# RWKV5 attention and a SwiGLU feed-forward layer on one core: VectorE's attention work of a late step in one line between the pieces, a quarter's silu products and later sums of h on GpSimd, and another order of the projections

## The chip, the cores and the metric

The kernel runs on one core of a Trainium2 chip. The core has a matrix engine (TensorE, PE in the profile, with its weight loads as PEld), a vector engine (VectorE, DVE), an activation engine (ScalarE, ACT), GpSimd (POOL), and a sync engine (SP), which in this kernel only issues DMAs. TensorE writes to PSUM, eight banks here; VectorE and ScalarE read PSUM and SBUF, and GpSimd is given work in SBUF alone. Each engine takes its instructions in the order in which the program emits them and waits at each for what it needs from the others. The metric is the device time of one execution in microseconds (us), the median of several.

## The reference

Two layers follow each other, all in float32. The first is a linear attention with a decaying state, over 4 batches, 8 heads, 768 positions and a head size of 48:

```
for t in range(S):
    cur = u * k_t (x) v_t
    y_t = r_t @ (state + cur)
    state = w * state + k_t (x) v_t
```

Its result, 3072 tokens by 384, goes into a feed-forward layer with 1536 hidden columns:

```
g = x @ w_gate
out = (silu(g) * (x @ w_val)) @ w_out
```

## The kernel before

**Attention.** The sequence is cut into chunks of 128 positions, one chunk of one batch to a step: 24 steps. From step 12 on (`PAIRED`) a step holds half a chunk of two batches at once. Step s works on several of them: it scales k and r for s+1 (`scale_k`, `scale_r`: GpSimd, L353 and L356), forms r·k·u for s+1 (`own_begin` L264, `own_end` L267: GpSimd) and its sum over a head (`own_sum` L275: VectorE), spreads that sum on diagonals (`diagonal` L376: eight ScalarE activations, which stand in a queue `small`), moves blocks of the scaled k and r (`move_blocks` L435: eight DMAs of SP's queue) and turns them (`turn_blocks` L456: two VectorE transposes, kT and rT). At one place in the step, called the *visit* in this document, TensorE does the outputs of s−2 (`paired_outputs` L557), the scores of s−1 (`paired_scores` L523) and the state update of s−2 (`paired_update` L571). Scores leave four masked copies for VectorE (L531), the update four sums into the state (L587), each second one followed by a product with the decay on GpSimd (L590). These eight wait in a deque `lazy`. `fill_turned` (SP) and `fill_own` (ScalarE's queue) are DMAs that fill the other parts of the score matrix `At`. Scores and update share four PSUM banks, the *ring*: a step takes three of the four in turn, so the second bank of this step's scores is the first bank of the last step's, and the third and fourth state sum read it.

**The feed-forward layer** is the bulk of TensorE's work, and it is cut into *pieces* that are fed between the parts of attention: a list `todo`, from which `feed` takes one at a time. With each piece `feed` also takes one from `lazy` (two while more than six are left) and up to three from `small`. From step 12 on, `gaps` feeds ten pieces in a step, two in each of five gaps: two pieces come before the visit and eight after it. One feeding is called a *turn* here, 1 and 2 before the visit, 3 to 10 after it. `turn_blocks` transposes kT after turn 3 and rT after turn 4; the sums of the state are taken in turns 6 to 9; the own sum comes ahead of turn 1 of the next step.

A *block* g = 2, 4, 6 holds 512 tokens (g and g+1, 256 each). Gate and value of a block come from `three_beside`: the 1536 columns are done in four quarters t = 0 to 3 of three tiles each, and each quarter is a fast multiplication of 15 products, *rounds* r0 to r14 (`three_step`, L924: four matmuls each). GpSimd forms the weight sums for it (`w_forms`, L854, and `in_place`, L827), VectorE the sums of x (`x_forms`, L881). Rounds add up in chains in PSUM: a bank is read out by VectorE or ScalarE (L948, called through `later`) after one round and then added to by the next of its chain, so the next must wait until the reading is done. These readings go to rows of `hv`: gates in their place, values in six rows at `place`. When a quarter is complete, ScalarE applies silu to its gates (L955) and a product with the values follows, for tile i = 0 and 1 on VectorE and for i = 2 on GpSimd (all L948); in quarter 3 there is one such product for each g instead, 128x768, the second as late as project 01. Quarter 1 has its values in rows 6 to 11, the other three in rows 0 to 5, so the readings of quarter 3 overwrite what the products of quarter 2 read.

The output projection is the 2x2 scheme with seven products, pieces "jn" of `two_projections`: j is the member of the pair, n the product (`project`, L740: twelve matmuls). Products 2 to 6 but 5 read sums of h (`h_sums`: L713 and L714 for the first pair of sums, L716 and L717 for the second). Their results are read out by ScalarE (L746, L750) and VectorE (L748, L753, L756) into two banks a and b of each g, b being written by product 1 and again by product 4 after L748 has read it. Product 1 reads tiles 6 to 11 of the first half of the tokens.

Pieces of one block fall on steps so: in steps 13, 17, 21 quarter 0 and most of quarter 1; in 14, 18, 22 the rest of it and quarter 2; in 15, 19, 23 the end of quarter 3 in turns 1 to 6 with project 00 in turn 5, then 10, 01, 02 and 11; in 16, 20, 24 the other projections 04 and 03 ahead of the visit, 12 and the rest after it, with the next block's first rounds between. Blocks 8 and 10 follow behind the last step in a scheme of their own (from about 436 us in the profile).

Of the kernel before, what the change touches and what calls it, by code (L numbers as in the profile page):

```python
# [15 lines left out]
P = 128  # L16
# [6 lines left out]
def fast(  # L23
# [419 lines left out]
                        ),  # L443
                    )

    def turn_blocks(i):

        turned[i] = three.tile([P, HP, P], FP32, name="rT", tag="rT")
        merged = hats[:, 6:8].rearrange("p n h x -> p (n h x)").rearrange(
            "p (q n a x) -> p n q a x", q=4, n=2, a=HP  # L450
        )
        for n, (dst, src) in enumerate(((kT[i % 2], blocks[0]), (turned[i], blocks[1]))):
            if i < PAIRED:
                dve.transpose(dst[:].rearrange("p a (t q) -> p q a t", q=4), merged[:, n])
            else:
                dve.transpose(dst[:].rearrange("p a t -> p (a t)"), src)  # L456
            if dst is kT[i % 2]:
                feed(1)

    lazy = deque()  # L460

# [242 lines left out]
    def h_sums(g, n):  # L704
        h11, h12, h21, h22 = h_quarters(g)
        if g < THREES:
            t = three.tile([P, 2, FH, P], FP32, name="hs", tag="w_bits")
        else:
            t = room["hs"][2 * (g % 2) + n]
        x = part_of.setdefault(g, {})  # L710
        x["s"] = x.get("s", ()) + (t[:, 0], t[:, 1])
        if n == 0:
            dve.tensor_add(t[:, 0], h22, h21)  # L713
            dve.tensor_sub(t[:, 1], t[:, 0], h11)  # L714
        else:
            dve.tensor_sub(t[:, 0], h11, h21)  # L716
            dve.tensor_sub(t[:, 1], h12, x["s"][1])  # L717

    def project(g, n):

# [218 lines left out]
    def three_beside(g):  # L939
# [18 lines left out]
        for t in range(4):  # L958
# [8 lines left out]
            if t < 3:  # L967
# [43 lines left out]
            later(at["r8"] + 0.1, dve.tensor_add, c[3], c[3], "l8")  # L1011
            give(at["r8"] + 0.2, "l8")
            if t < 3:
                for i, on in enumerate((dve, dve, pool)):
                    silu(
                        *((z + 11.7, z + 11.8) if i == 2 else (z + 15.6 + i / 10, z + (16.2, 22.1)[i])),
                        hTs[:, :, 3 * t + i], values[:, :, i], on,
                    )
# [391 lines left out]
    round_act()  # L1410
    load(6)
    for s in range(4, N + 2):
        if 4 < s < N:
            own_sum(s)
        if PAIRED <= s < N:
            diagonal(s)
        late = BLOCKS < s + 1 < N and s % 2 == 0
        if s + 3 == PAIRED:
# [7 lines left out]
            turn(s)  # L1426
        if s + 1 < N:
            scale_k(s + 1)
            if s < LATE:
                if not late:  # L1430
                    scale_r(s + 1)
                own_product(s + 1)
                if s + 1 < BLOCKS:
                    load_v(s + 1)
                if s + 3 < N and not late:
                    load(s + 3)
        if s + 1 < BLOCKS:
            turn(s)
        gaps(s, 0)
# [2 lines left out]
        if 4 <= s - 1 < N:  # L1442
# [17 lines left out]
        if PAIRED <= s < N:  # L1460
            fill_turned(s)
        if late or LATE <= s < N - 1:
# [3 lines left out]
        if BLOCKS <= s + 1 < N:  # L1466
            move_blocks(s + 1)
            if s + 1 < PAIRED:
                load_v(s + 1)
        if late and s < LATE and s + 3 < N:  # L1470
            load(s + 3)
        gaps(s, 2)
        if LATE <= s < N - 1:
            own_begin(s + 1)
            if s + 3 < N:
                load(s + 3)
        if 4 <= s - 2 < LATE - 2:
            outputs(s - 2)
            update(s - 2)
# [452 lines left out]
```

## Time and profile before

| | |
|---|---|
| median of 3 runs | 598.51 us (597.54 to 599.5) |
| the profiled execution | 601.09 us, span from first to last instruction 599.3 us |
| mean granted TensorE clock | 0.994 |
| instructions | 13566 |
| HBM read, written | 28.31 MB, 4.72 MB |

The profile gives for each engine the time in which it was busy; matmuls are pipelined, so a busy TensorE isn't one at its peak. A timeline row has start and duration in us, engine, line of the kernel, operation, the tiles written and read, and in brackets how long the engine was idle before it and what it waited for. A row of waits has the engine and line that waited, the engine and line waited for, the total in us, the number of waits and the longest. A row of windows has, for each engine, busy time and the number of instructions, then the granted TensorE clock as a share of the full one, the share of the DMA engines, and GB/s. A group row has count, busy time, mean duration in ns, and the idle time ahead of it.

### The profile page before, as it was taken

How to read it: one execution, taken by the hardware profiler on the slowest of the kernel's cores; microseconds unless marked ns; L12 is line 12 of the kernel's file. 1: busy time of each engine (PE TensorE's matmuls, PEld its weight loads, DVE VectorE, ACT ScalarE, POOL GpSimd, SP SyncE). 2: the span in 40 equal slices, each digit the busy share in tenths (PEclk: the TensorE clock that was granted, in tenths of full speed). 3: DMA queues.
4: the chain of work that ended last, by engine and by line, in shares of the span. 5: the costliest groups of instructions: out<-in, count | busy, mean ns of one | idle time of the engine just before them, and what ended most of it. 6: DMA issues, size and time to landing. Idle time of an engine off the chain costs nothing.

```text
span 599.3 us, 13566 instructions
## 1 busy us (share of the span) xinstructions
PE 575.3 (96%) x5370; PEld 514.1 (86%) x5370; DVE 448.8 (75%) x761; ACT 222.2 (37%) x529; POOL 365.5 (61%) x376
## 2 busy tenths in 40 slices
PE   8999999999999899999898999999999999999996
PEld 6788888899877688988788988888988899988896
DVE  7977776487678699497969767979747778377672
ACT  4658885331343422234331234351134420143410
POOL 5888888997998312979503579715778970011610
PEclk9999999999999899999999999999999999999999
DMA  7999967744534143562414452410110000200002
GB/s 197 228 243 240 299 197 77 107 71 94 116 58 84 30 84 70 115 109 41 79 36 77 101 117 40 76 33 19 29 27 1 0 2 1 54 0 1 2 2 55
DMA packets 151734, 48.09 MB, mean 80 GB/s; under 512 B 139313, under 2 KB 142386, under 8 KB 151666
## 3 DMA queue, kind: packets, MB, share of 16 engines
q1 hardware_dynamic: 147218, 40.69, 32.8%
q10 hardware_dynamic: 4448, 6.49, 3.8%
q8 instruction: 43, 0.70, 0.5%
q14 instruction: 25, 0.20, 0.1%
HBM read 28.31 MB, written 4.72 MB: 55 GB/s over the span
## 4 chain that ended last, share of the span: by engine, by line
PE 68%; DVE 16%; POOL 8%; DMA 3%; ACT 2%; issue 2%; SPq 0%; DVEq 0%; ACTq 0%; POOLq 0%
PE bank L924 18%; PE ring L924 13%; PE bank L665 10%; PE bank L740 9%; PE bank L1152 8%; DVE hv L948 6%; POOL s L854 3%; POOL wgv L827 2%; PE ring L622 2%; DVE At L531 2%; PE ring L557 2%; DMA v_ld<-in_v_dram 2%; PE ring L471 1%; DMA At<-zs 1%; PE ring L1152 1%
## 5 line engine op out<-in xcount | busy, mean ns | idle before, releaser
L948 DVE TENSOR_TENSOR hv<-hv,bank 128x512 f32<-128x512 f32 x132 | 86.9, 685 | 32.0 <-PE bank L924 23.3
L590 POOL TENSOR_TENSOR v_ld<-v_ld,w 48x384 f32<-48x384 f32 x20 | 20.5, 1024 | 76.8 <-DVE v_ld L587 71.7
L665 PE MATMUL bank<-xT,wgv 128*128 128x256 f32 x288 | 66.3, 384 | 0.0
L948 ACT COPY hv<-bank 128x512 f32<-128x512 f32 x72 | 40.3, 587 | 68.7 <-PE bank L924 52.0
L924 PE MATMUL bank<-xf,wgv 128*128 128x256 f32 x256 | 65.7, 381 | 0.0
L665 PEld LDWEIGHTS bank<-xT,wgv 128*128 128x128 f32 x288 | 53.4, 190 | 8.2 <-POOL wgv L228 0.2
L924 PEld LDWEIGHTS bank<-xf,wgv 128*128 128x128 f32 x256 | 48.0, 190 | 6.8 <-DVE kT L1197 0.6
L1206 POOL TENSOR_TENSOR hv<-At,hats 128x512 f32<-128x512 f32 x8 | 10.2, 1275 | 65.6 <-ACT At L1205 65.6
L924 PE MATMUL bank<-xT,s 128*128 128x256 f32 x152 | 39.2, 407 | 6.2 <-ACT hv L948 5.2
L854 POOL TENSOR_TENSOR s<-wgv 128x256 f32<-128x256 f32 x39 | 29.5, 776 | 24.5 <-PE bank L740 24.5
L924 PEld LDWEIGHTS bank<-xT,s 128*128 128x128 f32 x152 | 30.7, 205 | 12.7 <-issue 6.5
L955 ACT ACTIVATE hv<-hv 128x512 f32<-128x512 f32 (+1 forms) x33 | 21.2, 669 | 53.4 <-DVE hv L948 53.4
L924 PE MATMUL bank<-xT,wgv 128*128 128x256 f32 x144 | 36.0, 383 | 2.7 <-DVE hv L948 2.7
L740 PE MATMUL bank<-wo,hs 128*128 128x192 f32 x192 | 34.1, 328 | 2.6 <-DVE hv L748 2.6
L376 ACT ACTIVATE zs<-mask,du 128x64 f32<-128x64 f32 x96 | 25.5, 341 | 29.9 <-DVE du L275 19.4
L740 PE MATMUL bank<-wt,hs 128*128 128x192 f32 x192 | 34.3, 329 | 2.0 <-DVE hs L714 2.0
L740 PEld LDWEIGHTS bank<-wo,hs 128*128 128x128 f32 x192 | 31.6, 190 | 3.6 <-DVE hv L748 3.5
L740 PEld LDWEIGHTS bank<-wt,hs 128*128 128x128 f32 x192 | 31.2, 190 | 3.1 <-ACT hv L746 2.8
L924 PEld LDWEIGHTS bank<-xT,wgv 128*128 128x128 f32 x144 | 26.8, 190 | 7.7 <-DVE hv L948 4.5
L740 PE MATMUL bank<-wo,hv 128*128 128x192 f32 x192 | 33.3, 327 | 0.0
L740 PEld LDWEIGHTS bank<-wo,hv 128*128 128x128 f32 x192 | 31.7, 190 | 0.4
L854 POOL TENSOR_TENSOR s<-s 128x256 f32<-128x256 f32 x39 | 30.7, 786 | 1.0
(237 smaller groups left out, 1427.5 us busy)
## 6 DMA issues: line engine op xcount, KB each, us to landing
hats<-hats SPq DMA_DIRECT2D x96, 64.0 KB, 2.3
w_bits<-in_moe_w_gate_dram SPq DMA_DIRECT2D x6, 768.0 KB, 6.0
w_bits<-in_moe_w_val_dram SPq DMA_DIRECT2D x6, 768.0 KB, 6.8
w_bits<-in_moe_w_out_dram SPq DMA_DIRECT2D x6, 768.0 KB, 7.0
At<-zs ACTq DMA_DIRECT2D x24, 128.0 KB, 2.9
At<-rT SPq DMA_DIRECT2D x24, 128.0 KB, 2.4
v_ld<-in_v_dram SPq DMA_DIRECT2D x24, 96.0 KB, 6.0
k_ld<-in_k_dram SPq DMA_DIRECT2D x24, 96.0 KB, 3.0
```

Source lines behind the costliest of these rows:

```text
L376: lambda h=h: act.activation(own[:, i % 2, slot(i, h), :], ident64, AF.Identity, scale=du[:, h : h + 1])
L531: dve.copy_predicated(both(i)[rows, p, HP * g : HP * g + HP], m, ps[p][o : o + 64])
L557: pe.matmul(ps[32 * q : 32 * q + 32, cc, 64 * p : 64 * p + 64], *x, start=start, stop=stop, skip_group_check=True,)
L590: pool.tensor_mul(ze, ze, w.unsqueeze(3).to_broadcast([D, HP, 2, D]))
L622: pe.matmul(ps[32 * q : 32 * q + 32, cc, :], *x, start=start, stop=stop, skip_group_check=True,)
L665: pe.matmul(gv[:, o, :].rearrange("p (i t) -> p i t", i=2), wt[:, c, P * f : P * (f + 1)], xT[:, 2 * g % NX : 2 * g % NX + 2, c, :], start ...
L740: pe.matmul(ps, lhs[:, f, :], rhs[:, f, :], start=(f == 0 and n in (0, 1, 4)), stop=(f == FH - 1), skip_group_check=True,)
L854: op(made[o], made[a], made[b])
L924: pe.matmul(ps[:, o], u[:, o], v, start=first and o == 0, stop=True, skip_group_check=True,)
L948: do(out, *(pair_of(wide[a][:]) if isinstance(a, str) else a for a in args))
L955: todo.append((at, lambda: act.activation(gate, gate, AF.Silu)))
L1152: pe.matmul(ps, (h[what][q] if h[what] is D_ else h[what][:, q])[:, f, :], wide["o"][what][:, f, :], start=first and f == 0 and (split or ...
```

## The change

1. From step 12 on, VectorE's attention work of a step stands in one line in `lazy`, put together by a new function `after_visit` behind the scores: two masked copies, the transpose of kT, the third copy, the transpose of rT, the fourth copy, the own sum of the next step with its diagonal, and the four state sums. With the transpose of rT go `fill_turned`, `scale_r`, `move_blocks` and `load`. `feed` takes two only while more than nine are left, so that with eleven in line turn 3 takes both copies and turns 4 to 10, 1 and 2 one each: kT in turn 4, rT in 6, the own sum in 8, the state sums in 9, 10, 1, 2. The feeding inside `turn_blocks` goes back to its gap.
2. `own_begin` and `own_end` of step s+1 come at the start of step s, behind `scale_k`.
3. The values of quarter 2, not of quarter 1, lie in rows 6 to 11.
4. Quarter 2's products for i = 0 and 1 run on GpSimd, at other times.
5. The second pair of sums of h (L716, L717) runs on GpSimd for the blocks 2, 4 and 6.
6. In these blocks project 11 comes ahead of 02.

```diff
+    def turn_block(i, n):
+        if n == 0:
+            turned[i] = three.tile([P, HP, P], FP32, name="rT", tag="rT")
+        dst = (kT[i % 2], turned[i])[n]
...
+        else:
+            dve.transpose(dst[:].rearrange("p a t -> p (a t)"), blocks[n])
+
+    def after_visit(s):
+        def turn_second():
+            turn_block(s, 1)
+            fill_turned(s)
+            if s + 1 < N:
+                scale_r(s + 1)
+                move_blocks(s + 1)
+                if s + 3 < N:
+                    load(s + 3)
+        def own_term():
+            own_sum(s + 1)
+            diagonal(s + 1)
+        masked, sums = list(lazy)[:4], list(lazy)[4:]
...
+        lazy.clear()
+        lazy.extend([
+            *masked[:2], lambda: turn_block(s, 0), masked[2], turn_second, masked[3],
+        ])
+        if s + 1 < N:
+            lazy.append(own_term)
+        lazy.extend(sums)
...
         else:
-            dve.tensor_sub(t[:, 0], h11, h21)
-            dve.tensor_sub(t[:, 1], h12, x["s"][1])
+            on = dve if g < FIRST else pool
+            on.tensor_sub(t[:, 0], h11, h21)
+            on.tensor_sub(t[:, 1], h12, x["s"][1])
...
-        order = "00 10 01 02 11 04 03 12 05 06 13 14 15 16".split()
+        order = (
+            "00 10 01 11 02 04 03 12 05 06 13 14 15 16" if FIRST <= g < THREES else
+            "00 10 01 02 11 04 03 12 05 06 13 14 15 16"
+        ).split()
...
-            place = NR + (6 if t == 1 else 0)
+            place = NR + (6 if t == 2 else 0)
...
-                for i, on in enumerate((dve, dve, pool)):
+                for i, on in enumerate((dve, dve, pool) if t < 2 else (pool,) * 3):
+                    then = (16.2, 22.1) if t < 2 else (18.2, 20.2)
...
-            for _ in range(min(len(lazy), 1 + (len(lazy) > 6))):
+            for _ in range(min(len(lazy), 1 + (len(lazy) > 9))):
...
-                share[0] // 5 + (n < share[0] % 5) - (n == 1 and BLOCKS <= s < N),
+                share[0] // 5 + (n < share[0] % 5) - (n == 1 and BLOCKS <= s < PAIRED),
...
-            if s < LATE:
-                if not late:
-                    scale_r(s + 1)
-                own_product(s + 1)
+            if s < PAIRED and not late:
+                scale_r(s + 1)
+            own_product(s + 1)
...
                 load_v(s)
+                after_visit(s)
             gaps(s, 1)
-        if BLOCKS <= s < N:
-            turn_blocks(s)
-        if PAIRED <= s < N:
-            fill_turned(s)
...
-        if LATE <= s < N - 1:
-            own_begin(s + 1)
-            if s + 3 < N:
-                load(s + 3)
...
-        if LATE <= s < N - 1:
-            own_end(s + 1)
```

More of the change, by code (lines that the diff above doesn't have):

```diff
@@ L444, in move_blocks @@
                     )
[L446 to L458, printed above, removed]
+    def turn_block(i, n):
+        if n == 0:
+            turned[i] = three.tile([P, HP, P], FP32, name="rT", tag="rT")
+        dst = (kT[i % 2], turned[i])[n]
+        if i < PAIRED:
+            merged = hats[:, 6:8].rearrange("p n h x -> p (n h x)").rearrange(
+                "p (q n a x) -> p n q a x", q=4, n=2, a=HP
+            )
+            dve.transpose(dst[:].rearrange("p a (t q) -> p q a t", q=4), merged[:, n])
+        else:
[13 more added lines that the diff above has]
+        masked, sums = list(lazy)[:4], list(lazy)[4:]
+        if len(masked) < 4:
+            masked = [*masked, *(lambda: None for _ in range(4 - len(masked)))]
+        lazy.clear()
[5 more added lines that the diff above has]
+        lazy.extend(sums)
     lazy = deque()
@@ L1412, in fast @@
     for s in range(4, N + 2):
[L1413 removed]
+        if 4 < s <= PAIRED:
             own_sum(s)
[L1415 removed]
+        if s == PAIRED:
             diagonal(s)
@@ L1428, in fast @@
             scale_k(s + 1)
-            if s < LATE:
-                if not late:
-                    scale_r(s + 1)
-                own_product(s + 1)
-                if s + 1 < BLOCKS:
-                    load_v(s + 1)
-                if s + 3 < N and not late:
-                    load(s + 3)
+            if s < PAIRED and not late:
+                scale_r(s + 1)
+            own_product(s + 1)
+            if s + 1 < BLOCKS:
+                load_v(s + 1)
+            if s < PAIRED and s + 3 < N and not late:
+                load(s + 3)
         if s + 1 < BLOCKS:
@@ L1456, in fast @@
                 load_v(s)
+                after_visit(s)
             gaps(s, 1)
-        if BLOCKS <= s < N:
-            turn_blocks(s)
-        if PAIRED <= s < N:
-            fill_turned(s)
-        if late or LATE <= s < N - 1:
+        if BLOCKS <= s < PAIRED:
+            turn_block(s, 0)
+            feed(1)
+            turn_block(s, 1)
+        if late and s < PAIRED:
             scale_r(s + 1)
@@ L1469, in fast @@
                 load_v(s + 1)
-        if late and s < LATE and s + 3 < N:
+        if late and s < PAIRED:
             load(s + 3)
         gaps(s, 2)
-        if LATE <= s < N - 1:
-            own_begin(s + 1)
-            if s + 3 < N:
-                load(s + 3)
         if 4 <= s - 2 < LATE - 2:
```

4 lines of the change are left out of this document (2 added, 2 removed).

## The prediction

> **What bounds the kernel now.** I read the page first, then the waits of TensorE in the late steps, then the timelines around the longest wait.
>
> ```profile
> PE 575.3 (96%) x5370; PEld 514.1 (86%) x5370; DVE 448.8 (75%) x761; ACT 222.2 (37%) x529; POOL 365.5 (61%) x376
> 145.00:241.00 96.00, 89.71 (x900) 78.97 (x899) 75.73 (x121) 30.75 (x78) 58.64 (x72) 0.98 0.40 76
> 241.00:338.00 97.00, 91.75 (x925) 81.84 (x925) 77.41 (x127) 31.59 (x80) 55.38 (x65) 0.98 0.41 79
> 338.00:436.00 98.00, 95.75 (x989) 86.22 (x987) 74.73 (x126) 30.24 (x73) 67.29 (x75) 1.00 0.27 55
> PE bank L924 <- ACT hv L948: 5.2, 2, 2.6
> PE bank L924 <- DVE hv L948: 3.7, 7, 1.1
> PE bank L740 <- DVE hv L748: 2.6, 3, 1.0
> PE bank L740 <- DVE hs L714: 2.0, 3, 0.7
> ```
>
> TensorE (PE) is the bound: busy 96%. The second to fourth rows are the three blocks g = 2, 4, 6 (columns: PE, PEld, VectorE, ScalarE, GpSimd, granted clock). The last four rows are all its waits there, 13.5 us in 15 places; no matmul is removed, so only these and what follows them can be won. Two waits make 5.2 us:
>
> ```profile
> 253.80 2.75 PE L924 MATMUL bank<-xT,s 128*128 128x256 f32 x12
> 299.25 4.35 PE L924 MATMUL bank<-xT,s 128*128 128x256 f32 x12 [2.60 <-ACT hv L948]
> 202.69 4.51 PE L924 MATMUL bank<-xT,s 128*128 128x256 f32 x12 [2.60 <-ACT hv L948]
> 298.51 0.59 ACT L948 COPY hv<-bank 128x512 f32<-128x512 f32 x1 [3.12 <-DVE hv L948]
> 294.44 3.99 DVE L948 TENSOR_TENSOR hv<-hv 128x512 f32<-128x512 f32 x1 [0.39 <-ACT hv L955]
> 270.74 0.72 DVE L948 TENSOR_TENSOR hv<-hv 128x512 f32<-128x512 f32 x1
> 294.19 0.82 POOL L590 TENSOR_TENSOR v_ld<-v_ld,w 48x384 f32<-48x384 f32 x1 [0.39 <-PE bank L924]
> ...
> 296.89 0.99 POOL L264 TENSOR_TENSOR rk<-r_ld,k_ld 128x384 f32<-128x384 f32 x1
> 298.00:302.00 4.00, 2.75 (x7) 2.25 (x8) 2.79 (x5) 1.31 (x4) 0.00 (x0) 0.61 0.02 6
> 174.00:180.00 6.00, 4.89 (x140) 3.90 (x139) 3.72 (x6) 3.02 (x10) 5.77 (x9) 1.00 0.01 3
> ```
>
> The third quarter's first silu product takes 3.99 us, where such a product takes 0.72 at 270.74, because GpSimd runs four instructions (L590 to L264; L353 and L356 between) without a gap until 297.88 and VectorE gets in only then. ScalarE's copy of r12 writes the rows of `hv` that this product still reads, so it waits 3.12 us, and r9, which adds to the same bank, waits 2.60. Then the granted clock falls to 0.61, and twelve matmuls take 4.35 and 4.51 us instead of 2.75.
>
> Of the clock, the Trainium skill (TensorE: Matmul & The Clock Gate, Part 1: The HAM clock gate) says that it halves after about 3.4 us of idleness. Here 2.60 us did it; by the page these two waits would cost no clock, and the sum below would be 3.4 us smaller, 593.9 us.
>
> **The change part by part.** I number the ten turns of a step 1 to 10: 1 and 2 before the visit (outputs and scores), 3 to 10 after it. The step classes repeat every four: A (13, 17, 21) has quarters 0 and 1, B (14, 18, 22) 1 and 2, C (15, 19, 23) the end of quarter 3 and the first projections, D (16, 20, 24) the other projections.
>
> *Third quarter's products on GpSimd, values in other rows: −8.6 us.*
>
> ```profile
> 316.40 0.95 DVE L713 TENSOR_TENSOR hs<-hv 128x768 f32<-128x768 f32 x1
> 262.79 1.27 POOL L948 TENSOR_TENSOR hv<-hv 128x512 f32<-128x512 f32 x1 [2.71 <-ACT hv L955]
> 434.03 2.63 POOL L1066 TENSOR_TENSOR wo<-wo 128x1152 f32<-128x1152 f32 x1
> 319.27 1.51 POOL L590 TENSOR_TENSOR v_ld<-v_ld,w 48x384 f32<-48x384 f32 x1 [21.39 <-DVE v_ld L587]
> ```
>
> The 3.99 us instruction leaves VectorE, and quarter 3 no longer writes the rows that it read. Both waits go, 2 × 2.60, and the slow matmuls, 1.60 + 1.76: 8.56 us. On GpSimd two products of 1.27 us each start in turn 1 of C, some time after 297.88, where GpSimd was idle for 21.39 us until 319; they are read at 316 (L713). If GpSimd were stuck behind an L590 they would be late by its wait, but the L590 ahead of them waits for a sum that comes a turn earlier.
>
> *The same rows for quarters 0 and 1: +1.8 us.* Now quarter 1's ScalarE copies wait for quarter 0's products. For the second product of block 4 (0.72 at 270.74):
>
> ```profile
> 270.13 0.69 DVE L948 TENSOR_TENSOR hv<-hv,bank 128x512 f32<-128x512 f32 x1 [0.34 <-ACT hv L948]
> 166.89 1.28 DVE L948 TENSOR_TENSOR hv<-hv 128x512 f32<-128x512 f32 x1 [0.44 <-ACT hv L955]
> 270.37 1.08 ACT L948 COPY hv<-bank 128x512 f32<-128x512 f32 x2 [0.28 <-PE bank L924]
> 271.84 2.68 DVE L948 TENSOR_TENSOR hv<-hv,bank 128x512 f32<-128x512 f32 x4
> 272.76 1.89 PE L924 MATMUL bank<-xT,wgv 128*128 128x256 f32 x8
> ```
>
> The second row is block 2's first product. In block 4 the copies of r11 can start at 271.46 and end at 272.54, r6's sum ends at 273.2, and r7, which adds to its bank and now runs at 272.76, waits 0.5 us. In block 2, where GpSimd is busier and a product takes 1.28, I take 0.8: 0.5 + 0.5 + 0.8. From below nothing (VectorE may come earlier), from above the whole 4.3 us three times: a rival.
>
> *VectorE's attention work spread over the turns: −3.3 us.*
>
> ```profile
> 175.45 1.99 PE L924 MATMUL bank<-xT,wgv 128*128 128x256 f32 x8 [1.11 <-DVE hv L948]
> ```
>
> Of the seven waits on L948, 3.7 us, this one is in block 2: r6's sum stands behind the own sum (L275), which waits for GpSimd; the own sum moves to turn 8, and its products, L264 and L267, to the start of the step. The six others have two transposes and three copies just ahead of them in VectorE's queue; now a round's sums come between. I keep one of 0.45, where the transpose of rT takes the place of a state sum: 3.7 − 0.45 = 3.25. What is late next is the other end of the list: the state sums come in turns 9, 10, 1 and 2 instead of 6 to 9.
>
> *State sums just ahead of the visit: +2.1 us.* The third and fourth (0.36 us each) read the ring bank that this visit's scores write.
>
> ```profile
> 269.43 0.36 DVE L587 TENSOR_TENSOR v_ld<-ring,v_ld 48x192 f32<-48x192 f32 x1
> 274.69 0.69 DVE L948 TENSOR_TENSOR hv<-bank,hv 128x512 f32<-128x512 f32 x1 [0.17 <-PE bank L924]
> 274.58 1.11 PE L557 MATMUL ring<-At,v_ld 112*32 112x64 f32 x64
> 275.62 0.69 PE L523 MATMUL ring<-rT,kT 48*64 48x64 f32 x32
> ```
>
> Into B, turn 2 ends with r4's sum at 275.38, the fourth state sum would end at 275.75 at the earliest, and the scores start at 275.62: with what the third pushes back, 0.35 us, twice. Into D the fourth stands behind two x sums (L881) that GpSimd's run L590, L353, L264 can hold: between 0.2 and 3.3 us (3.99 − 0.72), I take 0.6 twice and 0.2 in step 24, which has no such run. Into A and C the last turn leaves VectorE less, and I take nothing: 0.7 + 1.4.
>
> *Order of projections, and the later sums of h on GpSimd: −0.1 us.*
>
> ```profile
> 313.74 4.06 PE L740 MATMUL bank<-wo,hv 128*128 128x192 f32 x24
> 318.49 2.19 PE L740 MATMUL bank<-wt,hs 128*128 128x192 f32 x12 [0.68 <-DVE hs L714]
> 323.58 2.22 PE L740 MATMUL bank<-wo,hs 128*128 128x192 f32 x12 [0.96 <-DVE hv L748]
> 319.13 0.96 DVE L948 TENSOR_TENSOR hv<-hv 128x768 f32<-128x768 f32 x1
> 320.00 1.59 DVE L716 TENSOR_TENSOR hs<-hv 128x768 f32<-128x768 f32 x1
> 323.19 0.34 DVE L748 TENSOR_TENSOR hv<-hv,bank 128x192 f32<-128x192 f32 x1
> POOL s L854 <- PE bank L740: 24.5, 4, 9.3
> ```
>
> Before, 02 waits 0.68 for L714 and 04 0.96 for L748, which stands behind L716 and L717; with three blocks that is 2.6 + 2.0 = 4.6 us, and it goes. But 11, now ahead of 02, reads the last product (319.13). Two state sums (0.72) leave the queue ahead of it, the rT transpose and the last copy come between L714 and it instead of ahead of both, and L717 on GpSimd beside it can hold it: it ends near 320.3. Half of 11's matmuls need nothing of it and fill 317.8 to 318.8; the rest waits 1.5 us, in three blocks 4.5. From below 0 (−4.6 in all), from above 1.5 with a clock loss of 1.65 each. A sum of 128x768 on GpSimd lies between 1.27 (128x512) and 2.63 (128x1152): 1.8 by the line between. Four a block are hidden: the first two end by 320 and are read at 325 or later, the other two run in D, where GpSimd's next weight sums wait up to 9.3 us for PE; without that cover these would be late by up to 7.2 us (4 × 1.8).
>
> *At nothing:* L264 and L267 at the start of the step are GpSimd's same work earlier, and no PE wait above is for GpSimd, so the weight sums that they push back come in time; if not, 2 us a step. The two fill DMAs, eight move DMAs and four loads on SP's queue go out two turns later, and what they bring is due eight of a step's ten turns after that; beyond that PE pays the overrun. ScalarE's eight diagonal activations come earlier, beside PE's rounds.
>
> **Sum.** −8.56 − 3.25 − 0.1 + 1.8 + 2.1 = −8.0 us. The profiled execution took 601.09 us (span 599.3); it comes to 593.1. It is 2.6 above the median of the runs, so I take the 8.0 from the median: 598.5 − 8.0 = **590.5 us**.
>
> **The rivals.** *The wait moves to quarters 0 and 1 (slower).* There r12's copy waits for quarter 0's first product, in class A, where GpSimd is busiest. If GpSimd holds that product as it did at 294.44, each block pays 2.6 + 1.7, 12.9 us instead of 1.8: 590.5 + 11.1 = 601.6. It decides once the product is held for 0.9 us beyond its 0.72: from 294.44 it would have ended at 295.16 and the copy behind it (0.59) at 295.75, and r9 was due at 296.65 (299.25 − 2.60). Against it: in class A, between GpSimd's short weight sums, 0.72 and 1.28 are what the rows show. The Trainium skill (SBUF — State Buffer, Who interferes with whom) says that a VectorE instruction with two inputs in SBUF and a GpSimd instruction block each other for a whole instruction, whoever comes first: the trace agrees (the L590 of 1.51 us beside 0.82). 0.10.
>
> *The wait for the last product costs clock too.* 1.5 us lies between a wait of 1.11 at 175.45 (granted 1.00) and 2.60. Three times 1.7: 595.6. 0.12.
>
> *Late state sums eat the gain.* If each of nine visits waits 1.0 us, 9.0 instead of 2.1: 597.4. For it: they stand directly behind what the last turn leaves. Against it: the outputs' 1.04 us cover most. 0.10.
>
> *It doesn't do what it says.* The long wait stays, with another instruction held in its place: −8.56 falls away, 599.1. 0.08.
>
> **How the numbers follow.** The forecast, 587 to 594.5, has 0.60. A measurement tells 0.3%, 1.8 us, from no change: faster 0.60 + 0.12 = 0.72, within it 0.10 + 0.08 = 0.18, slower 0.10. The range goes from 586, if the new waits nearly vanish, to 598, which takes in the second and third rival.
>
> **What would show it.** In the changed profile: no PE wait of 2.6 us in 190 to 300 and a clock of 1.00 there; no VectorE L948 of 3.99; waits of 11 for VectorE's 128x768 product of 1 to 2 us; waits of L523 for L587 under 0.5 us; r7 or r9 of quarter 1 waiting under 1 us. A PE wait over 2 us with a clock below 0.9 after it would make the prediction wrong.

## The result, and the profile after

| | before | after |
|---|---|---|
| median | 598.29 us (597.54 to 599.5, 4 runs) | 593.57 us (593.26 to 594.37, 4 runs) |
| profiled execution | 601.09 us, span 599.3 | 593.40 us, span 591.7 |
| granted clock in the profiled execution | 0.994 | 0.999 |

The ratio of the medians is 0.9921, with a 95% interval of 0.9902 to 0.9941: faster by about 0.8%. A second time, on another chip, after had 594.20 us beside 599.67 of before (0.9905, 0.9876 to 0.9933): 5.5 us. Between the two profiled executions the gain is 7.7 us, between the medians 4.7; the first experiment is about this gap.

In the changed kernel the lines are shifted: L924 is L953, L948 is L977, L740 is L766, L713 to L717 are L738 to L743, L748 is L774, L587 and L590 are L612 and L615, L523 is L548, L881 is L910, L854 is L883. L376 stays. First the page's busy time of each engine:

```profile
PE 572.1 (97%) x5370; PEld 513.0 (87%) x5370; DVE 430.2 (73%) x743; ACT 223.1 (38%) x529; POOL 390.0 (66%) x394
```

18.6 us of VectorE's work are gone and 24.5 us more are on GpSimd. The windows of the three blocks (columns as before):

```profile
145.00:241.00 96.00, 91.62 (x921) 81.71 (x919) 68.83 (x119) 32.34 (x81) 72.13 (x82) 1.00 0.42 82
241.00:338.00 97.00, 94.27 (x961) 84.71 (x964) 70.74 (x124) 34.75 (x90) 68.02 (x75) 1.00 0.43 81
338.00:436.00 98.00, 95.14 (x976) 85.30 (x965) 71.88 (x115) 29.68 (x66) 70.24 (x77) 1.00 0.27 52
```

The clock is 1.00 in all three, where it was 0.98 in the first two. TensorE's waits there, by line:

```profile
PE bank L766 <- DVE hv L977: 5.2, 3, 1.7
PE bank L953 <- DVE hv L977: 3.0, 3, 1.8
PE bank L953 <- ACT hv L977: 1.1, 3, 0.4
```

The two waits of 2.60 us are gone, and so are those for L714 and L748. Three new groups of three stand in their place, one wait of each group to a block. A tenth, of 0.43 us, is described with diagonal_later below. In the timeline of the second block:

```profile
265.53 0.88 DVE L977 TENSOR_TENSOR hv<-hv 128x512 f32<-128x512 f32 x1
266.50 1.07 ACT L977 COPY hv<-bank 128x512 f32<-128x512 f32 x2 [1.60 <-DVE hv L977]
267.61 1.88 DVE L977 TENSOR_TENSOR hv<-hv,bank 128x512 f32<-128x512 f32 x3 [0.81 <-ACT hv L977]
268.35 1.99 PE L953 MATMUL bank<-xT,wgv 128*128 128x256 f32 x8 [0.62 <-DVE hv L977]
291.36 1.13 PE L953 MATMUL bank<-xf,s 128*128 128x256 f32 x4 [0.37 <-ACT hv L977]
309.32 1.81 POOL L743 TENSOR_TENSOR hs<-hv,hs 128x768 f32<-128x768 f32 x1 [9.48 <-DVE hs L739]
310.30 1.64 DVE L977 TENSOR_TENSOR hv<-hv 128x768 f32<-128x768 f32 x1
312.00 1.24 PE L766 MATMUL bank<-wo,hv 128*128 128x192 f32 x6 [1.74 <-DVE hv L977]
```

The first four rows are the row conflict of quarters 0 and 1: the product that reads quarter 0's values, ScalarE's copies that overwrite them, the sum behind the copies, and r7, which waits for the sum. The last three are project 11: GpSimd's sum of h runs beside VectorE's last product, which takes 1.64 instead of 0.96 us, and 11 waits 1.74 for it. The waits of 1.73 to 1.76 us, of which r7 in the first block has one, cost no clock here.

### The profile page after: what moved, and what is told of

Its sections match the earlier page's. It is cut to its first block, busy times and chain, and to the rows that moved or that the text cites. A ratio compares the mean times of both kernels' runs of the same rounds, so it can differ in the third digit from the quotient of the medians.

```text
span 591.7 us, 13558 instructions
## 1 busy us (share of the span) xinstructions
PE 572.1 (97%) x5370; PEld 513.0 (87%) x5370; DVE 430.2 (73%) x743; ACT 223.1 (38%) x529; POOL 390.0 (66%) x394
## 4 chain that ended last, share of the span: by engine, by line
PE 85%; DVE 9%; ACT 3%; issue 1%; POOL 0%; DVEq 0%; POOLq 0%; ACTq 0%
PE bank L953 27%; PE bank L766 14%; PE ring L953 13%; PE bank L690 11%; PE bank L1182 8%; DVE hv L977 3%; PE ring L647 3%; PE ring L582 2%; PE ring L496 2%; ACT hv L977 1%; PE ring L548 1%; PE ring L1182 1%; PE ring L405 1%; PE ring L596 1%; DVE xf L910 1%
## 5 line engine op out<-in xcount | busy, mean ns | idle before, releaser
L977 DVE TENSOR_TENSOR hv<-hv,bank 128x512 f32<-128x512 f32 x132 | 87.1, 683 | 42.3 <-PE bank L953 28.6
L953 PE MATMUL bank<-xf,wgv 128*128 128x256 f32 x256 | 65.7, 381 | 0.0
L977 ACT COPY hv<-bank 128x512 f32<-128x512 f32 x72 | 40.1, 584 | 58.2 <-PE bank L953 41.9
L953 PEld LDWEIGHTS bank<-xf,wgv 128*128 128x128 f32 x256 | 48.0, 190 | 6.8 <-DVE kT L1227 0.6
L953 PE MATMUL bank<-xT,wgv 128*128 128x256 f32 x144 | 35.9, 382 | 3.1 <-DVE hv L977 3.0
L766 PE MATMUL bank<-wo,hv 128*128 128x192 f32 x192 | 33.6, 328 | 5.2 <-DVE hv L977 5.2
L766 PEld LDWEIGHTS bank<-wo,hv 128*128 128x128 f32 x192 | 31.5, 190 | 6.5 <-DVE hv L977 6.1
L953 PE MATMUL bank<-xT,s 128*128 128x256 f32 x152 | 35.2, 380 | 0.0
L883 POOL TENSOR_TENSOR s<-wgv 128x256 f32<-128x256 f32 x39 | 30.4, 797 | 6.4 <-PE bank L766 6.4
L376 ACT ACTIVATE zs<-mask,du 128x64 f32<-128x64 f32 x96 | 26.1, 339 | 22.1 <-DVE du L275 19.2
L766 PE MATMUL bank<-wt,hs 128*128 128x192 f32 x192 | 34.1, 328 | 0.0
L766 PE MATMUL bank<-wo,hs 128*128 128x192 f32 x192 | 33.8, 326 | 0.0
L953 PEld LDWEIGHTS bank<-xT,wgv 128*128 128x128 f32 x144 | 26.7, 190 | 8.1 <-DVE hv L977 4.7
L953 PEld LDWEIGHTS bank<-xT,s 128*128 128x128 f32 x152 | 28.7, 190 | 4.3 <-POOL s L883 0.5
L977 POOL TENSOR_TENSOR hv<-hv 128x512 f32<-128x512 f32 x15 | 19.0, 1275 | 19.8 <-ACT hv L984 19.7
L766 PEld LDWEIGHTS bank<-wo,hs 128*128 128x128 f32 x192 | 31.7, 190 | 0.2
L766 PEld LDWEIGHTS bank<-wt,hs 128*128 128x128 f32 x192 | 31.4, 190 | 0.2
L883 POOL TENSOR_TENSOR s<-s 128x256 f32<-128x256 f32 x39 | 30.7, 787 | 1.0
```

Source lines behind the costliest of these rows:

```text
L376: lambda h=h: act.activation(own[:, i % 2, slot(i, h), :], ident64, AF.Identity, scale=du[:, h : h + 1])
L766: pe.matmul(ps, lhs[:, f, :], rhs[:, f, :], start=(f == 0 and n in (0, 1, 4)), stop=(f == FH - 1), skip_group_check=True,)
L883: op(made[o], made[a], made[b])
L953: pe.matmul(ps[:, o], u[:, o], v, start=first and o == 0, stop=True, skip_group_check=True,)
L977: do(out, *(pair_of(wide[a][:]) if isinstance(a, str) else a for a in args))
```

## The experiments

The medians are of 5 to 12 executions. The last column gives the time against before on the same chip, with its 95% interval.

| run | what it is | median us | ratio |
|---|---|---|---|
| before_again | before | 599.52 | 0.9992 (0.9969 to 1.0016) |
| rows_only | before + part 3 | 600.29 | 1.0015 (0.9996 to 1.0035) |
| rows_silu | before + parts 3, 4 | 592.99 | 0.9888 (0.9864 to 0.9912) |
| line_only | before + parts 1, 2 | 595.18 | 0.9928 (0.9901 to 0.9956) |
| line_and_rows | before + parts 1 to 4 | 596.11 | 0.9935 (0.9911 to 0.9959) |
| old_order | after − part 6 | 592.27 | 0.9881 (0.9856 to 0.9905) |
| sums_on_vector | after − part 5 | 593.72 | 0.9915 (0.9881 to 0.9948) |
| after_again | after | 594.20 | 0.9905 (0.9876 to 0.9933) |
| other_rows_old_order | old_order + rows in turn | 589.08 | 0.9818 (0.9793 to 0.9843) |
| sums_6_on_vector | that + the last block's sums on VectorE | 588.17 | 0.9815 (0.9791 to 0.9838) |
| diagonal_later | that + diagonals one piece later | 585.20 | 0.9766 (0.9745 to 0.9787) |
| diagonal_two_later | the same, two pieces | 584.05 | 0.9741 (0.9714 to 0.9768) |

### Before once more: how often is the clock lost?

> The kernel before, unchanged. The gain is 7.7 us between the two profiled executions but 4.7 us between the medians. Theory: in the executions of before that are timed without a profile, the two waits of 2.60 us with the clock loss behind them do not both occur each time; then the granted clock of those runs is .996 to .999 where the time is 597.5 to 598.5, and a second profile has one or none of the waits, a clock above .994 and a span below 598. Rival: the profile itself slows this kernel; then every run lists a clock of about .994, the new profile has both waits and is 2 to 3 us above the median again.

The second profile (601.71 us, span 599.9) has both waits again, so the theory's "not both each time" finds no support for the waits, and its span below 598 did not come:

```profile
PE bank L924 <- ACT hv L948: 5.2, 2, 2.6
```

```profile
202.00:206.00 4.00, 3.30 (x10) 2.75 (x11) 2.31 (x4) 1.86 (x5) 0.00 (x0) 0.73 0.00 0
299.00:303.00 4.00, 3.83 (x10) 3.08 (x11) 1.82 (x3) 1.00 (x5) 0.00 (x0) 0.57 0.02 6
```

Here both waits cost clock as well, and the profile lies 2.2 us above the median again, as the rival has it. But the rival is wrong too: the clock isn't 0.994 in every run, and a profile need not be slow (after's is 0.2 us below its median, old_order's 0.55). Of 67 executions of before on four chips, 17 have 0.994 and take 601.0 us on the mean, 13 have 0.998 and take 597.6, the others lie between and a few beyond (0.986 with 604.07). So executions differ by what follows the waits: some lose the clock and some don't; the last section shows on what this depends. 0.004 of 599 us of lost clock is 2.4 us, and the two groups lie 3.4 apart. (The mean clock is no exact count of it: it also takes in what is lost behind the last matmul, 1.5 us in the profile of rows_only.) That the waits themselves stand in every execution I infer from both profiles; the timed executions list only the clock.

### Which part removes the two waits?

rows_only is the kernel before with the first two lines of this diff, rows_silu with all of it. line_only is the kernel after with all of it put back, and with the sums of h and the order as in before. Part 4 without part 3 was not run, so whether the rows are needed beside the products stays open.

```diff
-            place = NR + (6 if t == 1 else 0)
+            place = NR + (6 if t == 2 else 0)
...
-                for i, on in enumerate((dve, dve, pool)):
+                for i, on in enumerate((dve, dve, pool) if t < 2 else (pool,) * 3):
+                    then = (16.2, 22.1) if t < 2 else (18.2, 20.2)
                     silu(
-                        *((z + 11.7, z + 11.8) if i == 2 else (z + 15.6 + i / 10, z + (16.2, 22.1)[i])),
+                        *((z + 11.7, z + 11.8) if i == 2 else (z + 15.6 + i / 10, z + then[i])),
```

> Before with only the third quarter's values in the other rows and its silu products on GpSimd. Theory: both 2.60 us waits and the half clock behind them are gone (-8.6 on the profiled 601.1), and the waits between quarters 0 and 1 come (+1.8 to +3.0): profiled 594.3 to 595.5, no PE wait above 2 us between 190 and 300 us, clock 1.00 there; the median is then between 592 and 596, the more so the more often the waits occur in timed runs of before. Rival, that the line in one is what removes the starvation: both waits stay and the time is 598 or more.

> After with rows, silu products, sums of h and order put back: only VectorE's attention work stays in one line between the pieces. Theory: the alpha/beta waits go (-3.25), the state sums ahead of the visit cost nothing, as in after, and the waits for the third quarter's product stay wherever GpSimd still holds VectorE: 594 to 596 at the median, 1 to 1.5 us above after. Rival: with the line, VectorE's products no longer meet GpSimd's contiguous run, so that the 2.60 us waits go by this alone: 589 to 591, below after.

> Before with only the third quarter's values put in the other rows; all its silu products as before (two of three on VectorE). Theory: the other rows alone take the wait out of TensorE's way, since the copies of the fourth quarter no longer stand behind the held product: no wait of 2.6 us, the held product of about 4 us on VectorE may stay, time 592.5 to 594, like rows_silu. Rival: GpSimd's products are needed too, since VectorE is held just as long and its adds of the fourth quarter come late: a wait of 1.5 to 2.6 us stays near 200 and 295 us, 596 to 599.

rows_silu took 592.99, the theory's low end, and no wait over 0.96 us is left in its blocks. (Its profile took 595.48 us; it lost the clock once, near 19 us, far ahead of the blocks.) rows_only gained nothing, against the theory. Its timeline:

```profile
198.95 3.99 DVE L948 TENSOR_TENSOR hv<-hv 128x512 f32<-128x512 f32 x1 [0.39 <-ACT hv L955]
203.44 0.69 DVE L948 TENSOR_TENSOR hv<-hv,bank 128x512 f32<-128x512 f32 x1
204.27 1.97 PE L924 MATMUL bank<-xT,s 128*128 128x256 f32 x8 [2.24 <-DVE hv L948]
299.24 3.58 PE L924 MATMUL bank<-xT,s 128*128 128x256 f32 x8 [2.25 <-DVE hv L948]
```

The product is held for 3.99 us as before. ScalarE's copy no longer waits, but a sum of the fourth quarter on VectorE stands behind the product, and TensorE waits 2.24 us for that instead of 2.60 for the copy. So the other rows alone take 0.36 us off a wait; with the products moved to GpSimd as well, VectorE's queue is empty there. What held the product is shown by line_only, where the rows and products are those of before:

```profile
196.46 0.69 DVE L973 TENSOR_TENSOR hv<-hv 128x512 f32<-128x512 f32 x1 [0.25 <-ACT hv L980]
197.70 0.83 POOL L615 TENSOR_TENSOR v_ld<-v_ld,w 48x384 f32<-48x384 f32 x1 [2.72 <-DMA hats<-hats]
224.37 2.97 POOL L615 TENSOR_TENSOR v_ld<-v_ld,w 48x384 f32<-48x384 f32 x1 [19.14 <-DVE v_ld L612]
225.37 0.94 DVE L742 TENSOR_TENSOR hs<-hv,hs 128x768 f32<-128x768 f32 x1
226.68 0.94 DVE L906 TENSOR_TENSOR xf<-xT,xf 128x256 f32<-128x256 f32 x1
227.92 0.36 DVE L612 TENSOR_TENSOR v_ld<-ring,v_ld 48x192 f32<-48x192 f32 x1
228.33 0.62 PE L548 MATMUL ring<-rT,kT 48*64 48x64 f32 x26 [2.19 <-DVE v_ld L612]
323.15 0.62 PE L548 MATMUL ring<-rT,kT 48*64 48x64 f32 x26 [2.20 <-DVE v_ld L612]
```

With the line, GpSimd's run of attention work (first row of it at 197.70) comes only after the product, which takes 0.69 us, and the 2.60 us waits are gone without parts 3 and 4. Part 1 with 2, and part 3 with 4, remove the same waits; whichever comes second gets nothing for them. But line_only has the state sums late, which is what the prediction charged 2.1 us for: ahead of the visit of steps 16 and 20 the fourth state sum (227.92) stands behind the second sums of h (L742) and sums of x, and the scores wait 2.2 us. So line_only's 595.18 lies in the range of its theory by luck: the theory kept the waits that went and left out those that came. Those two waits also show that the clock isn't lost each time:

```profile
230.00:232.00 2.00, 2.00 (x8) 2.00 (x8) 1.95 (x4) 0.00 (x0) 1.83 (x2) 0.52 0.50 91
325.00:327.00 2.00, 2.00 (x14) 2.00 (x14) 1.95 (x5) 0.32 (x1) 1.66 (x2) 1.00 0.60 105
```

After 2.19 us the clock is 0.52, after 2.20 us in the next block 1.00. One thing more in line_only bears on the prediction. Its projections 02 and 04, with the old order and all sums of h on VectorE, wait for nothing:

```profile
311.49 2.19 PE L765 MATMUL bank<-wt,hs 128*128 128x192 f32 x12
315.49 2.22 PE L765 MATMUL bank<-wo,hs 128*128 128x192 f32 x12
```

In before they waited 0.68 and 0.96 us (318.49 and 323.58 there). The line alone takes these waits away.

### The line with the rows, the sums of h and the order

The diff goes from the kernel after. sums_on_vector has its first part, old_order its second, line_and_rows both.

```diff
-            on = dve if g < FIRST else pool
-            on.tensor_sub(t[:, 0], h11, h21)
-            on.tensor_sub(t[:, 1], h12, x["s"][1])
+            dve.tensor_sub(t[:, 0], h11, h21)
+            dve.tensor_sub(t[:, 1], h12, x["s"][1])
...
-        order = (
-            "00 10 01 11 02 04 03 12 05 06 13 14 15 16" if FIRST <= g < THREES else
-            "00 10 01 02 11 04 03 12 05 06 13 14 15 16"
-        ).split()
+        order = "00 10 01 02 11 04 03 12 05 06 13 14 15 16".split()
```

> After with the old projection order (02 before 11) in all blocks. Theory: project 11 no longer waits 1.74 us for the last 128x768 product three times (-5.2); project 02 waits about .7 for the sums of h instead (+2.1): 590 to 591. Rival: the wait moves whole, as 02 stands on the same VectorE line: 593 to 594, the sum of PE waits at the projection line still about 5.

> After with the second sums of h back on VectorE and the old order: the line in one together with rows and silu products. Theory: what took the state-sum wait of 2.2 us (line_only, twice) out of after is the second sums of h on GpSimd, which stood on VectorE just ahead of that visit; so it is back here, twice, with a clock loss in some runs, beside the waits between quarters 0 and 1 (3.0): 594 to 596, no better than rows_silu. Rival: the silu products alone give VectorE the room, no state-sum wait: 589 to 591.5.

> After with only the second sums of h back on VectorE, new order kept. Theory: the last 128x768 product is no longer held by GpSimd's sum (1.64 to .95 us), so project 11's three waits fall from 1.73 to about 1.0 (-2.1), but the state sums ahead of the late visit come late again (+4.4, twice 2.2): 595 to 596.5. Rival: the order alone makes that room, no state-sum wait: 591 to 592.

> The kernel after, unchanged, as the measure for the three runs beside it on this chip: 593 to 594.5, PE waits of 9 to 10 us between 140 and 440 us, granted clock .998 or more.

line_and_rows took 596.11 and has the state-sum wait of 2.20 us twice: the theory holds, and the line is a loss of 3 us beside rows_silu as long as the second sums of h stand on VectorE (on another chip; the intervals of the two ratios just overlap). With those on GpSimd (old_order) the two waits are gone and the time is 592.27. In sums_on_vector both things come as the theory said, the second at less than half the size:

```profile
218.41 0.96 DVE L976 TENSOR_TENSOR hv<-hv 128x768 f32<-128x768 f32 x1
219.42 1.24 PE L765 MATMUL bank<-wo,hv 128*128 128x192 f32 x6 [1.04 <-DVE hv L976]
228.82 0.39 PE L548 MATMUL ring<-rT,kT 48*64 48x64 f32 x10 [1.01 <-DVE v_ld L612]
```

The last product takes 0.96 again and project 11 waits 1.04 to 1.14, 2.0 us less in three blocks; the state sums come 1.0 us late, twice, 2.0 more. The time, 593.72, is after's. As I read it, the order that makes TensorE wait for the last product brings it later to the visit, and so VectorE less late. Of after_again's guesses the waits missed: its profile has 10.7 us of them. Old_order fits neither its theory nor its rival: it has no wait for the last product at all, and none of 02 for the sums of h, but a new one at the end of the last block:

```profile
412.40 6.21 DVE L907 TENSOR_TENSOR r_ld<-xT 128x256 f32<-128x256 f32 x1
412.69 1.81 POOL L742 TENSOR_TENSOR hs<-hv 128x768 f32<-128x768 f32 x1
414.47 1.81 POOL L743 TENSOR_TENSOR hs<-hv,hs 128x768 f32<-128x768 f32 x1
416.24 2.08 POOL L880 TENSOR_TENSOR s<-wgv 128x256 f32<-128x256 f32 x3
421.44 2.22 PE L766 MATMUL bank<-wt,hv 128*128 128x192 f32 x12 [1.56 <-ACT hv L772]
```

A VectorE sum of 128x256 stands from 412.40 to 418.61, beside GpSimd's L742, L743 and three L880 in a row, and all that VectorE has to do after it is late. (In sums_6_on_vector, below, such a sum takes 0.41 us.)

### A version without the new waits

other_rows_old_order is old_order with the two sets of rows in turn:

```diff
-            rows = hv[:, NR + 6 + 3 * (g % 2) : NR + 9 + 3 * (g % 2)].rearrange("p r t -> p (r t)")
+            o = NR + 3 * (g % 2) + 6 * ((g // 2 + 1) % 2)
+            rows = hv[:, o : o + 3].rearrange("p r t -> p (r t)")
...
-            place = NR + (6 if t == 2 else 0)
+            place = NR + 6 * ((g // 2 + 1 + t) % 2)
```

sums_6_on_vector is that with

```diff
-            on = dve if g < FIRST else pool
+            on = pool if FIRST <= g < THREES - 2 else dve
```

and diagonal_later is that with the diagonals behind the first state sum; diagonal_two_later has them behind the second.

```diff
-        def own_term():
-            own_sum(s + 1)
-            diagonal(s + 1)
+        def one_sum():
+            if sums:
+                sums.pop(0)()
+            diagonal(s + 1)
...
-            lazy.append(own_term)
+            lazy.extend([lambda: own_sum(s + 1), one_sum])
...
-        lazy.extend(sums)
+        lazy.extend(lambda: sums.pop(0)() for _ in sums[1:] if s + 1 < N)
+        if s + 1 >= N:
+            lazy.extend(sums)
```

> old_order with the two row sets taken in turn, so that no third's values share rows with the ones before or after them, nor with the projection's results. Theory: the waits of 1.77, .62 and .63 at the product between the first two quarters are the row conflict and go (-3.0): 589 to 590 beside old_order's 592.3. Rival: VectorE is late there for another reason and the waits stay: 592.

> other_rows_old_order with the second sums of h of the last pair of blocks (6 and 7) on VectorE. Theory: the one wait of 1.54 us left near 418 us came from a 128x256 VectorE operation held for some 6 us behind a row of GpSimd operations that these two sums open; it goes, and no state-sum wait comes as no visit follows: 587.3 to 588 beside 589.1. Rival: VectorE is late there from its own load, and 1.3 us more of sums make it worse: 589.5 to 591.

> sums_6_on_vector with the diagonal activations of the own term one piece later, the own sum where it is. Theory: ScalarE's copy of the fourth quarter no longer stands behind them, and the three waits of .37 go: 1.1 us less, 586.2 to 587. Rival: they collide with the next copies and silus of ScalarE instead: no gain or up to 1 us slower.

> diagonal_later with the diagonal activations a further piece later. In diagonal_later three of them (0.81 us) still stood between ScalarE's silus and its copies in the piece of the .37 wait, so the move by one piece was not the trial of it. Theory: with none of them in that piece the three waits of .37 go, 1.1 us less than diagonal_later: 584 to 584.8. Rival: the last of the eight come only just ahead of the next visit and the visit waits for the own term, 0.5 us or more at each of the late steps: 586 to 590.

With the rows in turn, block by block, the time is 589.08, and of the waits 1.77, .62 and .63 one is left, 0.47 in the first block:

```profile
174.74 1.56 PE L951 MATMUL bank<-xT,wgv 128*128 128x256 f32 x6 [0.47 <-DVE hv L975]
418.62 2.22 PE L767 MATMUL bank<-wt,hv 128*128 128x192 f32 x12 [1.54 <-ACT hv L773]
```

So the row conflict was their cause, for all but this 0.47. In sums_6_on_vector the wait of 1.54 us is gone, as the theory had it, and the time is 588.17 (586.96 to 589.15); its gain of 0.9 is no more than the two kernels' runs scatter, and its ratio's interval overlaps the one before it. In diagonal_later the waits of .37 stayed, since three diagonals were still in that piece:

```profile
288.78 0.81 ACT L376 ACTIVATE zs<-mask,du 128x64 f32<-128x64 f32 x3
289.50 1.05 ACT L978 COPY hv<-bank 128x512 f32<-128x512 f32 x2
290.11 1.13 PE L954 MATMUL bank<-xf,s 128*128 128x256 f32 x4 [0.37 <-ACT hv L978]
```

Its median fell by 3.0 us all the same. Two waits of 0.44 for ScalarE's copy of a projection went, which is 0.9; the rest isn't in its profile, whose own time is 588.24, with a wait of 1.74 us near 147 us and clock lost behind it. That wait is for a count that the kernel makes on VectorE at the end of step 12. The change doesn't touch the count, but its line puts the own sum ahead of it: none of the profiles without the line has this wait, and all ten with it do, 0.41 to 0.43 us in six and 1.73 to 1.75 in four (0.43 in after, 1.73 in after_again). The prediction has no term for it. How much of the 3.0 is how often it costs clock stays open; the profile of sums_6_on_vector has it at 1.74 with no clock lost. A piece later all three waits of .37 are gone: 584.05 (583.59 to 584.26), and one wait of 0.43 (that count) and one of 0.34 are all between 140 and 440 us. No visit waits for the own term. By 584.05 against 594.20 this version is 1.7% faster than after, measured on different chips.

## Why the prediction was right or wrong

It said 590.5 us, 587 to 594.5 if it went as forecast; 593.57 is in that. For the profiled execution it said 593.1, and that took 593.40.

**The step that failed is the last: "so I take the 8.0 from the median".** The 8.0 was made from an execution that had paid the full clock loss, and it was taken from a median of executions that mostly had paid less. Of the first term, 8.56, the 5.2 us of waiting stood in both profiles of before, but the 3.36 us of slow matmuls come in some executions. The sum would have had to be taken from the time that it was made against, or the clock term weighted; the 2.6 us between the two are nearly the whole of the 3.1 by which the forecast was too low. Part of the 2.6 is the base itself, a median of three executions: the 67 later ones, on four chips, have a median of 599.5.

**Quarter 2's products and rows, −8.6.** Both waits and the half clock are gone, as said. That the copy of r12 no longer waits isn't what does it (rows_only: 2.24 for 2.60); the held product has to leave VectorE, or GpSimd's run has to come at another time. And the term isn't the property of this part: line_only loses the same waits. The rival "the long wait stays, with another instruction held" is what rows_only does, at 600.29.

**Rows of quarters 0 and 1, +1.8.** Right in place and chain (product, copy, sum, r7), too small: 1.76, .62 and .63, 3.0 us. The first, in block 2, is the one most off, by 1.0 (in after_again it is 1.40), and it misses the sign "r7 or r9 of quarter 1 waiting under 1 us". In rows_silu, which has these rows without the line, the same three waits are 0.70, 0.45 and 0.43, near the 1.8 in sum (the first was 1.11 in before, behind the own sum). With the line and the rows they are larger: 1.43, 0.63 and 0.64 in line_and_rows. Why was not traced. The slower rival, a product held as at 294.44, did not come.

**VectorE's work spread, −3.25.** Six of the seven waits of before on that line are gone, the kept one of 0.45 too. The seventh, 1.11 at 175.45, stood at the r7 that the row conflict now holds, and in other_rows_old_order 0.47 us is left there. Against that, three of .37 for ScalarE came, from diagonals that the prediction put "beside PE's rounds" at nothing. They stood in front of the copies. 1.1 us; diagonal_two_later shows the cause. With the row conflict, the waits on this line are 4.1 us where 2.25 were predicted.

**State sums ahead of the visit, +2.1.** In after nothing. The mechanism is real, and larger into D than I took where the second sums of h are on VectorE (2.2 us for 0.6 in line_only; nothing into B), but part 5 takes away what delays them there. The prediction weighed the second sums of h only at the projections, and didn't follow them on to the next visit.

**Order and sums of h, −0.1.** The 4.6 us that this term counts as won are gone, but not by parts 5 and 6: line_only has none of these waits either. They belong to the line, and beside it part 6 wins nothing and brings 11's wait. Project 11 waits 1.73 for 1.5, three times, so the term is +0.6. The waits are those of the new order: old_order has none of them and is 1.3 us faster than the first measurement of after and 1.9 faster than the second (all on different chips). GpSimd's sum took the 1.81 us estimated (1.8) and held the product from 0.96 to 1.64.

These errors (+1.85, −2.1, +0.7) nearly cancel; that the sum for the profiled execution came within 0.3 us is in part luck. The next table takes each profiled execution, its PE waits of 0.2 us or more between 140 and 440 us, and what is lost in stretches of half the clock ahead of the last matmul, 1.71 us each (the last section shows them; in rows_only and rows_silu one is at the start, near 16 and 19 us). What is left should be the same for all.

| profiled execution | us | waits | half clock | left |
|---|---|---|---|---|
| before | 601.09 | 13.4 | 3.4 | 584.3 |
| before_again | 601.71 | 13.8 | 3.4 | 584.5 |
| rows_only | 601.05 | 13.2 | 3.4 | 584.5 |
| rows_silu | 595.48 | 8.2 | 1.7 | 585.6 |
| line_only | 594.77 | 7.1 | 1.7 | 586.0 |
| line_and_rows | 596.11 | 9.9 | 1.7 | 584.5 |
| after | 593.40 | 9.8 | 0 | 583.6 |
| after_again | 594.62 | 10.7 | 0 | 583.9 |
| old_order | 591.72 | 7.2 | 0 | 584.5 |
| sums_on_vector | 593.72 | 9.8 | 0 | 583.9 |
| other_rows_old_order | 588.96 | 4.4 | 0 | 584.6 |
| sums_6_on_vector | 588.17 | 3.7 | 0 | 584.5 |
| diagonal_later | 588.24 | 3.1 | 1.7 | 583.4 |
| diagonal_two_later | 584.09 | 0.8 | 0 | 583.3 |

What is left is 583.3 to 586.0 in all of them, where the times differ by 17.6: the time follows TensorE's waits and its clock, and VectorE's load alone decides nothing (in the three blocks it is busy for 211.5 us in after and for 224.0 in diagonal_two_later). Of the 7.7 us between the profiles of before and after, 3.6 are waits and 3.4 half clock.

## What to carry to other kernels

Where two edits remove the same wait, their gains don't add: look for what would be the next wait with the first edit alone, and count the second from there. A wait near the length at which the clock is lost costs its duration always and the slow matmuls only sometimes (here by where it falls on a grid of 3.41 us), so a sum made from one profile belongs to that profile's time, not to the median. Work that is moved to another engine frees its old queue at every later point too: follow the queue on to the next place where TensorE reads from it.

## What the runs showed of the hardware

The clock isn't lost at a fixed length of idleness. In line_only 2.19 us cost it and 2.20 us did not. In rows_only:

```profile
204.00:208.00 4.00, 3.73 (x124) 3.18 (x128) 2.61 (x5) 2.58 (x9) 0.00 (x0) 1.00 0.02 4
299.00:303.00 4.00, 3.76 (x24) 2.61 (x28) 2.52 (x5) 0.96 (x3) 0.00 (x0) 0.57 0.02 4
```

2.24 us at 204 cost nothing, 2.25 us at 299 brought 0.57. In after four waits of 1.73 to 1.76 cost nothing, but in diagonal_later, behind the wait of 1.74 us near 147:

```profile
149.00:153.00 4.00, 4.00 (x17) 4.00 (x16) 0.00 (x0) 1.15 (x4) 3.92 (x6) 0.64 0.57 112
```

What decides is when the wait falls. In all 14 profiles a loss of clock ahead of the last matmul is a stretch of 3.41 us at exactly half the clock, and the stretches of one execution start whole multiples of 3.413 us apart (in before at 203.34 and 298.92, 28 of them; in rows_only at 16.11 and 299.42, 83). So there is a fixed grid in time, and its place differs from one execution to the next. These windows are cut along it, the first number behind the comma being TensorE's busy time, for line_only and then for rows_only:

```profile
226.68:230.09 3.41, 1.76 (x64) 1.71 (x65) 3.35 (x6) 0.00 (x0) 3.25 (x4) 1.00 0.38 88
230.09:233.50 3.41, 3.41 (x13) 3.41 (x12) 3.33 (x7) 0.32 (x1) 1.74 (x2) 0.50 0.51 92
318.84:322.25 3.41, 2.12 (x74) 1.66 (x72) 3.34 (x6) 0.80 (x2) 2.98 (x2) 1.00 0.63 114
322.25:325.67 3.42, 2.52 (x69) 2.46 (x70) 3.34 (x8) 0.00 (x0) 3.34 (x4) 1.00 0.47 103
```

```profile
200.43:203.84 3.41, 1.60 (x8) 1.07 (x6) 3.38 (x3) 0.40 (x2) 1.96 (x3) 1.00 0.00 0
296.01:299.42 3.41, 1.16 (x6) 0.74 (x5) 3.38 (x4) 0.83 (x3) 1.35 (x2) 1.00 0.00 0
299.42:302.83 3.41, 3.41 (x12) 2.23 (x15) 1.93 (x4) 0.58 (x1) 0.00 (x0) 0.50 0.03 5
```

In line_only 1.65 us of the wait of 2.19 lie in one window, TensorE is busy for the other 1.76 us of it, and the next window has half the clock. The wait of 2.20 us is split between two windows, busy for 2.12 and 2.52 us, and nothing is lost. Cut so from 20 us to about 12 us ahead of the span's end, the 14 profiles have five windows in which TensorE is busy for 0.34 of the time or less, and each is followed by half the clock; no window over 0.52 is. Between 0.46 and 0.52 there are eleven, and three of them are followed by it (rows_only's first, 1.60 us, isn't); what decides there stays open, as the ends of matmuls in a trace are modelled.

The Trainium skill (TensorE: Matmul & The Clock Gate, Part 1: The HAM clock gate) calls the window in which activity is watched free-running and gives it 3413 ns; the grid in these traces agrees. Its rule that the clock is halved after one idle window, about 3.4 us, doesn't fit them: a window with TensorE idle for about half of it sufficed, in waits of 1.74 to 2.60 us.

A VectorE instruction with two inputs in SBUF was held for as long as GpSimd's instructions followed one another without a gap: 3.99 us behind four of them, 6.21 us beside the five quoted for old_order. It goes the other way too: in the rows above for line_only GpSimd's L615 at 224.37 took 2.97 us beside VectorE's sums of h and of x, where it took 0.83 at 197.70. The Trainium skill (SBUF — State Buffer, Who interferes with whom) calls the port pair that the two engines share an exclusive lock; that it isn't handed over between the instructions of a row is what these runs add.
